# Three moved steps in a gated mix of linear attention and single-expert retrieval: the last transposed coefficients, wo's last low part, and tile 1's sums of w

## The chip, the core and the metric

One NeuronCore of a Trainium2 chip runs the whole kernel. Its engines work side by side, each through its own instructions in order: TensorE (PE: matmuls out of SBUF into PSUM; PEld is its weight load), VectorE (DVE), ScalarE (ACT), GpSimd (POOL), and SyncE (SP), which here only issues DMAs. They wait for one another through semaphores. The metric is the device time of one execution in microseconds (us); less is better.

## The reference

For 2048 rows `x` of 512 numbers, two branches are mixed by a gate. `A_w_phi` is drawn 200 times larger than its plain scale.

```python
# A: linear attention, 32 heads of 16
q, k, v = split(x @ wqkv)
phi = lambda p: concat([softmax(p), softmax(-p)])     # 32 features
phi_q, phi_k = phi(q @ w_phi), phi(k @ w_phi)
kv = einsum("bhsf,bhsd->bhfd", phi_k, v);  z = sum_s(phi_k)
a = (phi_q @ kv / (phi_q . z + 1e-6)) @ wo
# B: 256 experts = 16 x 16, the best one per head
s1, s2 = q1 @ k1.T, q2 @ k2.T                         # per row and head
e = argmax(s1) * 16 + argmax(s2)
b = sum_over_heads( gelu(x . u[e]) * v[e] )           # softmax over one candidate is 1
g = sigmoid((x * gate_w).sum())
out = g * a + (1 - g) * b
```

As all heads share the experts' tables, `b` is, for each row, a count C of how often each of the 256 experts is chosen, times G = (1 - g) gelu(x . u), times the table `v`.

## The kernel before

**Tiles.** Rows are worked on in 16 tiles of 128 (a = 0 to 15). Numbers that go through a matmul are split into a high and a low part (`xh`/`xl`, `woh`/`wol`, `eh`/`el`, `ch`/`cl`), and three matmuls (high-high, high-low, low-high) make one product.

**Stages.** A first stage, up to about a third of the time, makes keys, values and the sums over all rows. The second is a software pipeline, written out by hand (`manual_schedule`: each engine takes its work in the order of the text). Pass a of the loop at L972 does the query softmax of tile a, the counting of tile b = a - 1 and the output of tile z = a - 2, and starts the scores of tile n = a + 1. The last tiles are written out behind the loop (L1080 to L1137).

**The steps by name.**

- `soft_in(a)` (L115 to L121, VectorE): the differences to maximum and minimum of the query projection; `soft_exp(a)` (L685, ScalarE): two exponentials; `soft_w(a)` (L691, POOL): w = phi times `zb`, two halves; `soft_sum(a, i)` (L695, VectorE): sums of phi; `soft_y(a, i)` (L705, VectorE): sums of w; `soft_p(a)` (L700, VectorE); `soft_b(a)` (L713 to L726): the factors on VectorE, with one step of a's own counting between each two of them, and the final products on POOL (L726). `planes` (L758), a DMA transpose and `join` (L768) turn phi; `mid_num` (L777, L781) makes the numerator and copies its high part to `xh`; `num_lo` (L788) makes the low part.
- `best(n, half)` (L734, L735, VectorE): row maximum of the scores and the places that equal it; `turn_eq`: their DMA transpose; `mid_mask` (L796, TensorE): bit masks of them.
- `count(t)` (L800): a generator of VectorE operations that turns the masks into C. `step(t, n)` runs the next n of its yields, `drain(t)` all that are left. L804 to L808 are the first five, L812 and L814 the sixth, L822 the seventh, L825 the eighth, and L826 to L836 follow.
- `gelu_in` (L653, POOL), `gelu_act` (L657 to L659, ScalarE), `gelu_out` (L663, POOL) make G. `coef` (L840) multiplies C by G, on POOL for all but the last two tiles. `c_planes` (L845, ScalarE, then a DMA transpose from SP) and `c_join` (L852, L856, ScalarE) turn the product and leave `ch`; `back_cl` (L877) makes `cl`. For the last two tiles `back_c` (L866, L868, L872) turns it on TensorE.
- `back(z)` runs `back_mm` (L882): 12 matmuls of the numerator with `woh`/`wol` (L889) and then 6 of the coefficients with `eh`/`el` (L896), into one bank `po`; `store` copies it out (L913) and writes it by DMA.

**`wo`.** `woh` and `wol` hold four parts each, in memory that earlier tables used (L879). Part 3 goes where `wbh` and `wbl`, the weights of `vproj`, lie, so it can be written only after `vproj(15)` in pass a = 1: its high part on ScalarE (L984), its low part on VectorE (L1005). Part 2's low part is on POOL (L1043).

**Order around the change, pass a = 1.** VectorE: `soft_in(1)`, L1005, three steps of tile 0's counting (L812 to L825), `best(2, 0)`, the two `soft_sum(1)`, the rest of tile 0's counting (L826 to L836), the two `soft_y(1)`, `soft_p(1)`, `soft_b(1)`. POOL: `soft_b(0)`'s products (L726), `gelu_in(1)`, `soft_w(1)`, `gelu_out(0)`, `coef(0)`. ScalarE: the planes of tile 0, `soft_exp(1)`, the copies of `kvb` (L919), `join(0)`, `c_planes(0)`, `gelu_act(1)`, and then in pass a = 2 the `xh` copies of tile 0, `gelu_pre(2)` and `c_join(0)` among tile 1's planes.

**Order at the end.** Tile 15's output is made in two halves of 256 columns, `end0` and `end1`, each with 12 matmuls L889 and 6 matmuls L896. All 24 L889 come first, then `back_c(15)`'s two transposes, ScalarE's `ch`, VectorE's `cl`, then the L896 of either half, with a copy and a DMA behind each.

Of the kernel before, what the change touches and what calls it, by code (L numbers as in the profile page):

```python
# [16 lines left out]
ALU = mybir.AluOpType  # L17
# [18 lines left out]
def mix_kernel(ctx, tc, xT, wqT, wkT, wv, wphi, wo, wq, kk, ug, ev, cst, out):  # L36
    nc = tc.nc
    pe, dve, act, pool, sp = nc.tensor, nc.vector, nc.scalar, nc.gpsimd, nc.sync
# [4 lines left out]
    def mm_bank(name):  # L43
        return psum.tile([P, 512], F32, tag="mm", bufs=4, name=name)
# [206 lines left out]
    def vproj(t, ks=range(NK)):  # L251
        pv = mm_bank(f"pv{t}")
        proj(pv, t, wbh, wbl, 0, D, ks)
        v = v_tile(t)
        return lambda: act.copy(v, by16(pv))
# [134 lines left out]
    def spare(src, name, shape):  # L390
        t_ = wa_.tile(shape, F32, tag="xr", bufs=4, name=name)
        sp.dma_start(t_, src)
        return t_
# [75 lines left out]
    for t in range(5, NT - 1, 2):  # L469
        n = t + 1  # L470
# [13 lines left out]
        a = pks[t] = mm_bank(f"pk{t}")  # L484
        prod(a, tile_of(t, 0), b11, True)
        b = mm_bank(f"pu{t}")
# [97 lines left out]
    rawo = {k: spare(wo[:, k], f"rawo{k}", [P, D]) for k in range(2)}  # L584
# [28 lines left out]
    def step(t, n=1):  # L613
        for _ in range(n):
            if t in chains and next(chains[t], None) is None:
                del chains[t]

    def drain(t):
        while t in chains:
            step(t)  # L620
# [22 lines left out]
    def gelu_pre(t):  # L643
        gelu_gate(t)
        gelu_rest(t)

    def gate(t):
        gs = st8[t]["g"]
        yield dve.reciprocal(gs[:, 2:3], gs[:, 1:2])

    def gelu_in(t):
        px, x2 = st8[t]["G"], st8[t]["x2"]
        pool.tensor_tensor(x2, x2, px, op=ALU.mult)  # L653
# [11 lines left out]
    def front_q(t):  # L665
        pq = mm_bank(f"pq{t}")
        proj(pq, t, wah, wal, 0, D)
        st8[t]["pq"] = pq
# [13 lines left out]
    def soft_exp(t):  # L682
        d = st8[t]["ph"]
        for i in range(2):
            act.activation(hs(d, i), hs(d, i), AF.Exp)  # L685
# [11 lines left out]
    def soft_p(t):  # L697
        st = st8[t]["st"]
        sm = pair(st[:, 64:128])
        dve.scalar_tensor_tensor(st[:, 128:224].rearrange("p (h c) -> p h c", c=3)[:, :, 2], sm[:, :, 0], 1e-6,  # L700
                                 sm[:, :, 1], op0=ALU.mult, op1=ALU.mult)
# [52 lines left out]
    def planes(t, i):  # L754
        e = st8[t]
        e.setdefault("tp", [])
        pl = w3.tile([P, 2, 512], U16, tag="pl", name=f"pl{i}_{t}")
        act.copy(pl, e["ph"][:, halves[i]].bitcast(U16).rearrange("p (c j) -> p j c", j=2))  # L758
        tp = w3.tile([P, 8, P], U16, tag="tp", name=f"tp{i}_{t}")
        sp.dma_start_transpose(tp, pl.rearrange("p j c -> p (j c)"))  # L760
        e["tp"].append(tp)
# [9 lines left out]
    def mid_num(t):  # L771
        e = st8[t]
        o = [tr_bank(f"oT{q}_{t}") for q in range(2)]
        for g in range(8):
            for q in range(2):
                r0, c0 = 64 * q, 32 * (g % 4)
                pe.matmul(o[q][c0:c0 + 32, (g // 4) * P:(g // 4 + 1) * P], kvb[r0:r0 + 64, g, :],  # L777
                          e["pt"][r0:r0 + 64, g, :], start=(g < 4), stop=True, skip_group_check=True)
        oh, ol = x_of(t)
        for q in range(2):  # L780
            act.copy(oh[:, 2 * q:2 * q + 2].rearrange("p k n -> p (k n)"), o[q][:, :2 * P])  # L781
        e["o"] = (oh, ol, o)

    def num_lo(t):
        oh, ol, o = st8[t]["o"]
        for q in range(2):
            k2 = lambda a: a[:, 2 * q:2 * q + 2].rearrange("p k n -> p (k n)")
            dve.tensor_tensor(k2(ol), o[q][:, :2 * P], k2(oh), op=ALU.subtract)  # L788
# [60 lines left out]
    def c_join(t):  # L849
        e = st8[t]  # L850
        tj = w4.tile([P, 2 * P], F32, tag="ctj", bufs=1, name=f"ctj{t}")
        act.copy(tj.bitcast(U16).rearrange("p (k n j) -> p j k n", j=2, n=P),  # L852
                 e["tc"].rearrange("p (j k) n -> p j k n", j=2))
        ch = w4.tile([P, 2 * P], F32R, tag="ch", name=f"ch{t}")
        cl = w4.tile([P, 2 * P], F32R, tag="cl", name=f"cl{t}")
        act.copy(ch, tj)  # L856
        if t == 0:
            w4.tile([P, 120], F32, name="rest4", bufs=1)
        e["c"] = (ch, cl, tj)
# [15 lines left out]
    def back_cl(t, eng=dve):  # L875
        ch, cl, o = st8[t]["c"]
        eng.tensor_tensor(cl, o[:, :2 * P], ch, op=ALU.subtract)  # L877

    woh, wol = ([a[:, 0], a[:, 1], b.rearrange("p k n -> p (k n)"), c[:, 0]]  # L879
                for a, b, c in ((t1h, gh, wbh), (t1l, gl, wbl)))  # L880
# [20 lines left out]
    def back(t, n=18):  # L901
        if t not in backs:
            split_ = DEFER - 2 <= t < NT - 3
            e = st8[t]
            e["po"] = psum.tile([P, 512], F32, tag="acc", name=f"po{t}") if split_ else mm_bank(f"po{t}")
            backs[t] = back_mm(t, bank=e["po"])
        for _ in range(n):
            next(backs[t])

    def store(t):  # L910
        po = st8.pop(t)["po"]
        ot = w3.tile([P, D], F32, tag="ot", name=f"ot{t}")
        act.copy(ot, po)  # L913
        sp.dma_start(out[t * P:(t + 1) * P, :], ot)
# [57 lines left out]
    for a in range(NT - 1):  # L972
        n, b, z = a + 1, a - 1, a - 2
        owed = min(18, 3 * max(0, a - DEFER))
        left = min(18, 3 * max(0, a - DEFER + 1))
        B, Z = b >= 0, z >= 0
        if Z:
            mid_num(z)
        if a == 2:
            gelu_pre(a)  # L980
        if a == 1:
            front_q(a)
            v15 = vproj(NT - 1)
            act.copy(woh[3], rawo[3])  # L984
        if B:
            planes(b, 0)
            if Z:
                c_join(z)
            if a == 1:
                v15()  # L990
            planes(b, 1)
        if a > 1:
            front_q(a)
        if owed:
            back(z - 1, owed)
            store(z - 1)
        gelu_in(a)
        if Z:
            num_lo(z)
        if B:  # L1000
            if a == 1:
                for _ in gate(a):
                    pass
                soft_in(a)
                dve.tensor_tensor(wol[3], rawo[3], woh[3], op=ALU.subtract)  # L1005
                step(b, 3)
            else:
                soft_in(a, dealt(a, b, z))
                drain(b)
        else:  # L1010
            for _ in gate(a):
                pass
        if a != 1:
            gelu_act(a)
        if a > 0:
            soft_exp(a)
        if Z and not left:
            back(z)
            store(z)
        if not left and a > 1:  # L1020
            mid_mask(a)
        if a:
            front_s(n, 0)
        if left or a == 1:
            mid_mask(a)
            if 0 < left < 18:
                back(z, 18 - left)
        if a == 1:
            kvacc(NT - 1)
            kv_final()  # L1030
            cl_.close()
            w4 = ctx.enter_context(tc_pool("w4", "right"))
        front_s(n, 1)
        front_p(n, False)
        soft_w(a)
        if a == 1:
            best(n, 0)
        soft_sum(a, 0)
        soft_sum(a, 1)
        if a == 1:  # L1040
            drain(b)
        if a == 0:
            pool.tensor_tensor(wol[2], rawo[2], woh[2], op=ALU.subtract)  # L1043
            step(a, 5)
        if a != 1:
            best(n, 0)
        if a == 0:
            best(n, 1)
            turn_eq(n)
        soft_y(a, 0)  # L1050
        soft_y(a, 1)
        soft_p(a)
        if B:
            join(b)
            gelu_out(b)
            coef(b)
            c_planes(b)
            if a == 1:
                gelu_act(a)
        if a == 0:  # L1060
            soft_b(a, lambda t: None)
        else:
            soft_b(a)
            best(n, 1)
            turn_eq(n)
        if a != 1:
            gelu_pre(n)
    a, b, z = NT - 1, NT - 2, NT - 3
# [19 lines left out]
    for _ in gate(a):  # L1088
# [34 lines left out]
    coef(a)  # L1123
    ends = [(back_mm(a, slice(256 * i, 256 * i + 256), o[:, :256]), o) for i, o in
            enumerate((mm_bank("end0"), mm_bank("end1")))]
    for g, _ in ends:
        for _ in range(12):
            next(g)
    back_c(a)
    back_cl(a)  # L1130
    ot = w3.tile([P, D], F32, tag="ot", name="ot_end")
    for i, (g, o) in enumerate(ends):
        for _ in range(6):
# [57 lines left out]
```

## Time and profile before

| | |
|---|---|
| time, median of 3 executions | 373.98 us (373.77 to 374.05) |
| the profiled execution | 373.71 us |
| its span in the profile | 371.9 us, 8839 instructions |
| TensorE busy | 365.0 us (98%) |
| VectorE busy | 332.6 us (89%) |
| ScalarE busy | 256.3 us (69%) |
| POOL busy | 203.1 us (55%) |
| chain that ended last | PE 83%, DVE 5%, POOL 3%, ACT 3%, issue 3%, DMA 2% |

The profile comes from one execution. A row of the timeline gives the start in us from the start of the span, the duration in us, the engine, the line, the operation, what it writes and reads, how many instructions are merged in it, and in brackets how long the engine was idle before and what ended that. A row's duration counts any time in which the operation had begun and was held up, so a row longer than others of its kind is a sign of a hold-up. Neighbouring rows of one engine may overlap by some hundredths of a microsecond, as instructions are pipelined; ends of matmuls are modelled. The span ends when the last output transfer has landed, some 2 us behind the last instruction; the execution's time is 1.8 us longer than the span.

### The profile page before, as it was taken

Reading aid. Unit: us, or ns where it says so; the run is one execution under the profiler, and the core shown is the slowest. Engines: PE = TensorE matmul, PEld = TensorE weight load, DVE = VectorE, ACT = ScalarE, POOL = GpSimd, SP = SyncE. Lnnn points to the kernel's source line nnn. Section 1 sums busy time; section 2 is a strip of 40 time slices with the busy share of each in tenths; the row PEclk is TensorE's granted clock in tenths of the full one; section 3 lists DMA queues with packets and bytes.
Section 4 is the critical chain, followed back from the end, with each engine's and each line's share of the span. In section 5 each row is a group of like instructions: output and inputs, shape, how many; then the busy total and the mean of one; then the engine's idle time right before and its main releaser. Section 6 shows DMA issues by size and latency. Waiting matters only on the chain.

```text
span 371.9 us, 8839 instructions
## 1 busy us (share of the span) xinstructions
PE 365.0 (98%) x3443; PEld 286.2 (77%) x3443; DVE 332.6 (89%) x786; ACT 256.3 (69%) x459; POOL 203.1 (55%) x205
## 2 busy tenths in 40 slices
PE   8999999999999999999999999999999999999995
PEld 4766767777878878777888888878878888888875
DVE  3679999999787979999989999999999999999993
ACT  4585577876666676677868659667786786777641
POOL 1079989988848846443634436426435445454700
PEclk9999999999999999999999999999999999999999
DMA  7868987557882304145264242351452532532201
GB/s 259 321 241 277 252 278 237 173 179 277 279 179 85 89 6 82 24 105 82 61 86 104 57 95 75 85 100 16 114 76 67 115 77 66 115 69 62 70 31 56
DMA packets 72074, 46.67 MB, mean 125 GB/s; under 512 B 63584, under 2 KB 64480, under 8 KB 69728
## 3 DMA queue, kind: packets, MB, share of 16 engines
q1 hardware_dynamic: 71168, 45.24, 45.5%
q10 hardware_dynamic: 864, 0.87, 0.9%
q8 instruction: 27, 0.44, 0.5%
q14 instruction: 15, 0.12, 0.1%
HBM read 26.43 MB, written 4.19 MB: 82 GB/s over the span
## 4 chain that ended last, share of the span: by engine, by line
PE 83%; DVE 5%; POOL 3%; ACT 3%; issue 3%; DMA 2%; SPq 0%; POOLq 0%; ACTq 0%; DVEq 0%
PE po L889 10%; PE s L56 7%; PE s L57 6%; PE s L58 6%; PE po L896 6%; PE pk L459 5%; PE pu L459 4%; PE ws L292 4%; PE pq L56 4%; PE pq L58 3%; PE pq L57 3%; PE oT L777 2%; PE pe L459 2%; PE kvacc L283 2%; PE pv L459 2%
## 5 line engine op out<-in xcount | busy, mean ns | idle before, releaser
L691 POOL TENSOR_TENSOR w<-d,zb 128x512 f32<-128x512 f32 x32 | 40.9, 1297 | 76.8 <-ACT d L685 76.8
L56 PE MATMUL s<-sh,xh 128*128 128x512 f32 x128 | 50.9, 397 | 0.0
L57 PE MATMUL s<-sl,xh 128*128 128x512 f32 x128 | 49.9, 390 | 0.0
L58 PE MATMUL s<-sh,xl 128*128 128x512 f32 x128 | 49.8, 389 | 0.0
L726 POOL TENSOR_TENSOR d<-d,st 128x512 f32<-128x512 f32 x30 | 31.2, 1062 | 28.1 <-DVE st L720 26.5
L685 ACT ACTIVATE d<-d 128x512 f32<-128x512 f32 x32 | 20.0, 632 | 34.2 <-DVE d L119 26.1
L276 POOL TENSOR_TENSOR d<-d,st 128x1024 f32<-128x1024 f32 x16 | 32.5, 2032 | 8.5 <-ACT d L267 6.6
L768 ACT COPY pt<-tp 128x1024 uint16<-128x1024 uint16 x28 | 36.3, 1369 | 0.0
L758 ACT COPY pl<-d 128x1024 uint16<-128x1024 uint16 x28 | 29.2, 1044 | 5.5 <-POOL d L726 5.4
L58 PEld LDWEIGHTS s<-sh,xl 128*128 128x128 f32 x128 | 24.0, 188 | 5.0
L56 PEld LDWEIGHTS s<-sh,xh 128*128 128x128 f32 x128 | 24.0, 188 | 4.7
L57 PEld LDWEIGHTS s<-sl,xh 128*128 128x128 f32 x128 | 24.1, 188 | 4.6
L56 PE MATMUL pq<-wah,xh 128*128 128x512 f32 x64 | 26.8, 418 | 0.0
L58 PE MATMUL pq<-wah,xl 128*128 128x512 f32 x64 | 25.1, 392 | 0.0
L57 PE MATMUL pq<-wal,xh 128*128 128x512 f32 x64 | 25.0, 390 | 0.0
L156 DVE TENSOR_TENSOR xl<-xr,xh 128x512 fp32r<-128x512 f32 (+2 forms) x17 | 21.7, 1288 | 1.7 <-ACT xh L152 1.6
L735 DVE TENSOR_TENSOR eq<-s,mx 128x512 bf16<-128x512 f32 x32 | 22.1, 691 | 1.1
L695 DVE TENSOR_REDUCE st<-d 128x32 f32<-128x512 f32 x32 | 21.5, 680 | 1.4
L734 DVE TENSOR_REDUCE mx<-s 128x32 f32<-128x512 f32 x32 | 21.8, 680 | 0.0
L705 DVE TENSOR_REDUCE st<-w 128x32 f32<-128x512 f32 x32 | 20.5, 677 | 0.6 <-POOL w L691 0.6
L271 DVE TENSOR_REDUCE st<-d 128x64 f32<-128x1024 f32 x16 | 19.4, 1209 | 1.8 <-ACT d L267 1.6
L267 ACT ACTIVATE d<-d 128x1024 f32<-128x1024 f32 x16 | 17.1, 1066 | 4.1 <-DVE d L121 4.1
(272 smaller groups left out, 1119.3 us busy)
## 6 DMA issues: line engine op xcount, KB each, us to landing
wq<-wq SPq DMA_DIRECT2D x16, 1024.0 KB, 5.8
xr<-xT SPq DMA_DIRECT2D x15, 256.0 KB, 5.1
y<-ot SPq DMA_DIRECT2D x15, 256.0 KB, 2.3
rawk<-wkT SPq DMA_DIRECT2D x1, 1024.0 KB, 6.5
rawq<-wqT SPq DMA_DIRECT2D x1, 1024.0 KB, 6.8
rawu<-ug SPq DMA_DIRECT2D x2, 258.0 KB, 5.2
rawv<-wv ACTq DMA_DIRECT2D x2, 256.0 KB, 4.7
rawv<-wv SPq DMA_DIRECT2D x2, 256.0 KB, 5.9
```

What stands on the lines that cost most here:

```text
L56: pe.matmul(o, ah, bh, start=(first and i == 0), stop=False)
L57: pe.matmul(o, ah, bl, start=False, stop=False)
L58: pe.matmul(o, al, bh, start=False, stop=(last and i == n - 1))
L276: pool.tensor_tensor(g64(d), g64(d), b64(st[:, 128:192]), op=ALU.mult)
L459: pe.matmul(o, x_, w_, start=(first and i + j == 0), stop=(i == 1 and j == 2), skip_group_check=True)
L691: pool.tensor_tensor(hs(e["w"], i), hs(e["ph"], i), hs(zb, i), op=ALU.mult)
L726: eng.tensor_tensor(g64(d)[:, gs_], g64(d)[:, gs_], r[:, gs_].unsqueeze(2).to_broadcast([P, 32, F]), op=ALU.mult)
L735: dve.tensor_tensor(e["eq"][:, 512 * half:512 * half + 512].rearrange("p (h f) -> p h f", f=F), p3, mx.unsqueeze(2).to_broadcast([P, H, F] ...
L758: act.copy(pl, e["ph"][:, halves[i]].bitcast(U16).rearrange("p (c j) -> p j c", j=2))
L768: act.copy(p16[:, :, 4 * i:4 * i + 4, :], e["tp"][i].rearrange("p (j g) n -> p j g n", j=2))
L889: pe.matmul(po, a, b, start=(i == 0), stop=False)
L896: pe.matmul(po, a, b, start=False, stop=(i == 5))
```

## The change

Three places, all of them moves of work that stays the same:

1. In pass a = 1, the low part of `wo`'s part 3 is made by POOL instead of VectorE, at the same place in the text: on POOL that is behind `gelu_in(1)` and ahead of `soft_w(1)`.
2. In pass a = 1, the rest of tile 0's counting (`drain(b)`) is moved from behind `soft_sum(1)` to behind `soft_y(1)` and `soft_p(1)`. It stays ahead of `join(0)`, `gelu_out(0)` and `coef(0)` in the text; these are on other engines.
3. At the end, the transposes of tile 15's coefficients, and ScalarE's and VectorE's work on them, come behind 18 of the 24 matmuls L889 instead of behind all 24; the remaining six, which belong to `end1`, follow the transposes on TensorE.

```diff
@@ -1002,7 +1002,7 @@
                 for _ in gate(a):
                     pass
                 soft_in(a)
-                dve.tensor_tensor(wol[3], rawo[3], woh[3], op=ALU.subtract)
+                pool.tensor_tensor(wol[3], rawo[3], woh[3], op=ALU.subtract)
                 step(b, 3)
             else:
                 soft_in(a, dealt(a, b, z))
@@ -1037,8 +1037,6 @@
             best(n, 0)
         soft_sum(a, 0)
         soft_sum(a, 1)
-        if a == 1:
-            drain(b)
         if a == 0:
             pool.tensor_tensor(wol[2], rawo[2], woh[2], op=ALU.subtract)
             step(a, 5)
@@ -1050,6 +1048,8 @@
         soft_y(a, 0)
         soft_y(a, 1)
         soft_p(a)
+        if a == 1:
+            drain(b)
         if B:
             join(b)
             gelu_out(b)
@@ -1123,11 +1123,13 @@
     coef(a)
     ends = [(back_mm(a, slice(256 * i, 256 * i + 256), o[:, :256]), o) for i, o in
             enumerate((mm_bank("end0"), mm_bank("end1")))]
-    for g, _ in ends:
-        for _ in range(12):
+    for (g, _), n in zip(ends, (12, 6)):
+        for _ in range(n):
             next(g)
     back_c(a)
     back_cl(a)
+    for _ in range(6):
+        next(ends[1][0])
     ot = w3.tile([P, D], F32, tag="ot", name="ot_end")
     for i, (g, o) in enumerate(ends):
         for _ in range(6):
```

## The prediction

> **What bounds the kernel now.** I first read which waits TensorE has at all, since its instructions run in the order written and it is busy for nearly the whole span. The view of waits, for TensorE alone, has five rows; three lie where the change touches the program (columns: who waits for whom, us in total, times, longest).
>
> ```profile
> PE po L889 <- ACT xh L781: 0.6, 1, 0.6
> PE po L896 <- ACT ch L856: 0.6, 1, 0.6
> PE end L896 <- ACT ch L872: 0.5, 1, 0.5
> ```
>
> The first two are in pass a = 2 (tile 0's output matmuls), the third at the very end. Everywhere between them TensorE waits for nobody, so a microsecond won or lost at one of these places should reach the end whole. What sets the first is in the chain of work that ended last, cut to that window (start, us, what):
>
> ```profile
> 152.01 0.44 DVE cf L836
> ...
> 152.61 0.75 POOL cf L840
> 153.38 0.62 ACT plc L845
> ...
> 155.07 0.65 ACT xh L781 x2
> ```
>
> ```profile
> 155.50 0.50 PE L889 MATMUL po<-t1h,xh 128*128 128x512 f32 x1 [0.61 <-ACT xh L781]
> ```
>
> The chain reads backwards: TensorE's `po` matmul needs ScalarE's copies `xh`. ScalarE takes its work in order too, so these copies stand behind `plc`, tile 0's `c_planes`; that waits for POOL's product L840, and this for L836, the last step of tile 0's counting on VectorE. So the end of the counting, at 152.45, sets TensorE's restart at 155.50. The wait for `ch` stands behind the same ScalarE work and moves with it.
>
> VectorE and POOL before that, from the timeline (start, us, engine, line):
>
> ```profile
> 143.50 0.67 DVE L121 TENSOR_TENSOR d<-st,pq 128x512 f32<-128x512 f32 x1
> 144.09 1.19 DVE L1005 TENSOR_TENSOR wbl<-rawo,wbh 128x512 fp32r<-128x512 f32 x1
> 145.21 0.21 DVE L812 TENSOR_TENSOR m<-sa 128x64 uint16<-128x64 uint16 x1
> 145.34 0.17 DVE L814 TENSOR_TENSOR m<-sa 128x32 uint16<-128x32 uint16 x1
> 145.54 0.43 DVE L822 TENSOR_TENSOR X<-m,m 128x256 uint32<-128x256 uint32 x1
> 146.00 0.29 DVE L825 TENSOR_SCALAR T<-X 128x256 uint32<-128x256 uint32 x1
> 146.21 0.68 DVE L734 TENSOR_REDUCE mx<-s 128x32 f32<-128x512 f32 x1
> ...
> 147.54 1.27 DVE L695 TENSOR_REDUCE st<-d 128x32 f32<-128x512 f32 x2
> 148.72 0.96 DVE L826 TENSOR_TENSOR X<-X,T 128x512 uint16<-128x512 uint16 x1
> ...
> 152.35 1.27 DVE L705 TENSOR_REDUCE st<-w 128x32 f32<-128x512 f32 x2
> ...
> 153.64 0.22 DVE L804 CAST sa<-mk 128x64 uint16<-128x64 f32 x1
> ```
>
> ```profile
> 139.13 1.28 POOL L1043 TENSOR_TENSOR gl<-rawo,gh 128x512 fp32r<-128x512 f32 x1
> ...
> 144.00 0.74 POOL L653 TENSOR_TENSOR x<-x,px 128x256 f32<-128x256 f32 x1
> 146.13 2.56 POOL L691 TENSOR_TENSOR w<-d,zb 128x512 f32<-128x512 f32 x2 [1.40 <-ACT d L685]
> 148.66 0.74 POOL L663 TENSOR_TENSOR px<-x,px 128x256 f32<-128x256 f32 x1
> ```
>
> VectorE has no idle time here, and two of its rows are too long: L1005 and L826. Each began while a POOL product was running (L653, L663) and ended shortly after it.
>
> **How the two engines block each other.** L1005 ends at 145.28, 0.54 after L653's end (144.74). L826 ends at 149.68, 0.28 after L663's end (149.40); its usual duration is the first number here:
>
> ```profile
> L826 DVE TENSOR_TENSOR X<-X,T x16: 424/426/960, 148.7 to 361.3; 128x512 uint16<-128x512 uint16 x16
> ```
>
> So a VectorE operation with two SBUF inputs waits for the POOL operation under way, and then needs its own duration less about 0.15 (0.43 - 0.28). Who comes next when both queue is shown early in the kernel; the last two rows give the lines' usual durations (ns: least, median, most):
>
> ```profile
> 37.75 3.03 DVE L156 TENSOR_TENSOR xl<-xr,xh 128x512 fp32r<-128x512 f32 x2
> 37.79 2.44 POOL L276 TENSOR_TENSOR d<-d,st 128x1024 f32<-128x1024 f32 x1
> 40.19 1.74 POOL L316 TENSOR_TENSOR sl<-wtj,sh 128x512 fp32r<-128x512 f32 x1
> ```
>
> ```profile
> L276 POOL TENSOR_TENSOR d<-d,st x16: 1932/1942/2470, 30.7 to 126.1; 128x1024 f32<-128x1024 f32 x16
> ```
>
> ```profile
> L316 POOL TENSOR_TENSOR sl<-wtj,sh x8: 1270/1295/1736, 40.2 to 119.0; 128x512 fp32r<-128x512 f32 x8
> ```
>
> The first L156 runs and L276 is 0.50 longer than its median; the second L156 waits for L276 and ends 0.55 after it (40.78 against 40.23); L316 is again 0.44 too long. They take turns, one instruction each, and whoever is waiting goes next.
>
> **Part 1: wol[3] on POOL.** VectorE loses L1005, 1.19. POOL gains one operation of L1043's shape and kinds, 1.28, between L653 and L691, where POOL is idle for 1.40 (144.74 to 146.13): alone, it would hide there. But three steps of tile 0's counting now follow `soft_in` directly, from 144.10, and L812, L814 and L822 each have two SBUF inputs. Step by step:
>
> - L812 waits for L653 and goes in at 144.74; 0.21 - 0.15 = 0.06, so it is done at 144.80. Then wol[3] has its turn, 1.28, to 146.05 or so (POOL rows overlap by some 0.03).
> - L814, next on VectorE, waits for that and is done at 146.07 (0.17 - 0.15). L822 begins 0.03 behind it, at 146.10, by a hair ahead of L691's 146.13. It takes its 0.43, to 146.53, and holds L691 up by some 0.20: the first L691 (1.28) ends at 147.61.
> - L825 comes at 146.55 and meets that L691. It has one input. No row shows such an operation beside POOL. Reductions with one input (L695 inside L691's 2.56) aren't lengthened: wait 0 is the lower end. The upper end is the two-input rule: to 147.61, then 0.29 - 0.15, done at 147.75. I take the upper end: L825 writes as many 32-bit elements as L822 in 0.29 instead of 0.43, on the same tile in SBUF, so it moves more than one per cycle, unlike the reductions (0.68 for 512), and needs more than one way to memory.
> - L734, best(2,0), begins 0.08 before L825's end, at 147.67 (146.21 now). Had nothing blocked, it couldn't begin before the scores, 145.66 + 0.39 = 146.05 below, so the removed 1.19 is worth 0.1 at most:
>
> ```profile
> 145.66 0.39 PE L58 MATMUL s<-sh,xl 128*128 128x512 f32 x1
> ```
>
> For L825 the Trainium skill, SBUF — State Buffer, section Who interferes with whom, says that tensor_scalar can enter a mode that uses both of VectorE's SBUF ports and then blocks with GpSimd for a whole instruction. By that rule the upper end is right and the sum is as below; by the reductions' rows it would be 0.95 less. The same section says that what issues first wins, which fits L653 and L812; the turns after it are from the rows above.
>
> **Part 2: the sums of w ahead of the rest of the counting.** From L734 to the end of the second L695 is 2.51 (146.21 to 148.72) and stays. Now come the two sums of w and `soft_p`: from L705's start to that of L804 behind them, 1.29. They don't wait: w's halves are written by about 147.6 and 148.9, and the sums start at 147.67 + 2.51 = 150.18. So L826 starts at 151.47. POOL's L663 is then over, and L826 takes 0.43 instead of 0.96: it ends at 151.90, against 149.68. From there the counting is as before: L836 ends, and L840, `plc`, `xh` and TensorE's L889 start, 2.22 later. The pieces: 1.46 (L734 late) + 1.29 (sums first) - 0.53 (L826 unblocked).
>
> Queued behind the late L840 on POOL are only tile 1's products L726, which wait for VectorE's steps behind the counting; these are late by less than 2.2, as VectorE's work between has become shorter. Behind `plc` on ScalarE stand `gelu_act(1)`, the `xh` copies, `gelu_pre(2)`, tile 1's planes with their transposes, and `c_join`, all late by 2.22, as TensorE is. No DMA is added or removed; the transpose of `plc` starts later by the same. **+2.22**.
>
> **Part 3: the last coefficients.** The end, from the timeline:
>
> ```profile
> 364.53 0.43 DVE L840 TENSOR_TENSOR cf<-cf,px 128x256 f32<-128x256 f32 x1
> 365.17 0.28 PE L889 MATMUL end<-gl,xh 128*128 128x256 f32 x1
> 365.89 0.28 PE L889 MATMUL end<-wbh,xl 128*128 128x256 f32 x1
> 366.01 0.38 PE L866 MATMUL CT<-cs,cf 128*128 128x128 f32 x2
> 366.49 0.37 ACT L872 CAST ch<-CT 128x256 fp32r<-128x256 f32 x1 [2.52 <-PE CT L866]
> 366.89 0.42 DVE L877 TENSOR_TENSOR cl<-CT,ch 128x256 fp32r<-128x256 f32 x1 [1.93 <-ACT ch L872]
> 366.91 0.39 PE L896 MATMUL end<-eh,ch 128*128 128x256 f32 x1 [0.52 <-ACT ch L872]
> 367.13 0.28 PE L896 MATMUL end<-el,ch 128*128 128x256 f32 x1
> ...
> 368.69 0.37 ACT L1136 COPY ot_end<-end 128x256 f32<-128x256 f32 x1 [1.83 <-PE end L896]
> ```
>
> The row at 365.17 is the 18th of the 24 matmuls, that at 365.89 the last: (365.89 - 365.17) / 6 = 0.12 each. The transposes go from 366.01 to 365.29; their input, L840, is done at 364.96, 0.33 earlier. Then `ch` goes to 365.77-366.14 and `cl` to 366.17-366.59. Six matmuls, 0.72, now fill what was the wait. Eight transposes elsewhere took 1.04:
>
> ```profile
> 357.87 1.04 PE L749 MATMUL pt<-cs,d 128*128 128x128 f32 x8
> ```
>
> So two take 0.26 of TensorE (their own row has 0.38, the upper end). L896 can begin at 365.29 + 0.26 + 0.72 = 366.27, behind `ch` (366.19 with its 0.05 of signal), and its second matmul at 366.39 instead of 367.13: 0.74 (0.62 by the upper end, never above 0.72 and the 0.10 that the restart costs, 367.13 - 366.91 against 0.12). The matmuls with `cl` come fifth, at 366.75, after 366.59. Copies and output DMAs behind move along. **-0.74**.
>
> **Sum.** +2.22 - 0.74 = +1.48. The profiled execution took 373.71 (span 371.9): 375.19. The median shown, 373.98, is 0.27 above it, so **375.5** on that scale.
>
> **Rivals.**
>
> *Worse turns.* L822 beats L691 by 0.03 of estimate. If L691 wins, L822 waits to 147.41 and is done at 147.69; the second L691 is held up and ends at 148.85, L825 at 148.99, L734 begins at 148.91: 1.24 more, +2.7, 376.7. For it: the hair's breadth; against it: if L814 slips in with L812, L822 waits for wol[3] alone and goes at its end, 146.05, clear of L691.
>
> *L825 doesn't wait.* L734 begins at 146.55 + 0.21 = 146.76, 0.91 earlier: +0.5 to +0.6, 374.5. For it: the one-input reductions; against it: the pace.
>
> *Blocking doesn't bite on such short steps* (the side that isn't slower). L812, L814 and L822 slip between L653 and wol[3], and wol[3] hides in POOL's 1.40. L734 begins at 146.10, L826 at 149.90, ending at 150.33: +0.65, and with the end -0.09: 373.9. It decides from the point where L734 begins before 146.2. Against it: the turns at 37.75 and L812's own 0.06, too short to keep POOL's next operation out for three instructions.
>
> *The end doesn't move.* If the last transposes wait for L840 past 366.0, part 3 gives nothing: +2.2, 376.2. Against it: 0.33 of margin.
>
> *Faster* would need the front to lose nothing, TensorE's restart at 155.50 not hanging on L836: -0.74, 373.2. Against it: ScalarE's `plc` starts 0.02 after L840's end.
>
> **How the numbers follow.** The forecast has 0.50 (with it the case that L814 slips in with L812: 0.1 less), worse turns 0.15, L825 not waiting 0.14, no blocking 0.10, the end not moving 0.05, faster 0.06. Differences within 0.2% (0.75 us) can't be told from none here. Faster: 0.06. Same: no blocking and most of L825 not waiting, 0.22. Slower: the rest, 0.72. The range, 374.2 to 376.9, takes in L825's two ends, the worse turns without a slower clock, and the end's 0.62 to 0.82; left out are no blocking and faster, 0.16.
>
> **What would show it.** In the new trace: L812 ending with L653, L814 some 1.2 later with wol[3], L825 stretched to about 1.2 beside L691; L826 at 0.43 and starting near 151.5; ScalarE idle before `plc` 2.2 longer; TensorE's wait for `xh` at 2.8 instead of 0.61. At the end, no wait before L896 and the last copy 0.7 earlier relative to the 18th matmul. I'm wrong if L734 begins before 147, or if TensorE's wait for `xh` stays under 1.5.

## The result, and the profile after

| | before | after |
|---|---|---|
| time, median of 7 executions each | 373.93 us (373.57 to 374.16) | 375.45 us (374.86 to 377.33) |
| ratio, with its 95% interval | | 1.0048 (1.0029 to 1.0067) |
| the profiled execution | 373.71 us | 374.91 us |
| its span | 371.9 us | 373.1 us |

The kernel became slower by about half a per cent, 1.5 us by the medians. The two profiled executions differ by 1.2. The changed kernel's seven executions also lie farther apart, and three of them (375.78, 376.08, 377.33) show a mean granted TensorE clock of 0.994 instead of 1.000; this turned out to belong to the change.

The waits of TensorE in the changed kernel (who waits for whom, us, times, longest):

```profile
PE po L889 <- ACT xh L781: 2.8, 1, 2.8
...
PE po L896 <- ACT ch L856: 0.6, 1, 0.6
```

The wait at the end has gone from the list; the one in pass a = 2 has grown from 0.6 to 2.8. VectorE in pass a = 1 (start, us, engine, line), where the reader is to compare the durations of L812, L814 and L825 with the 0.21, 0.17 and 0.29 of before:

```profile
143.37 0.68 DVE L121 TENSOR_TENSOR d<-st,pq 128x512 f32<-128x512 f32 x1
143.96 0.71 DVE L812 TENSOR_TENSOR m<-sa 128x64 uint16<-128x64 uint16 x1
144.60 1.29 DVE L814 TENSOR_TENSOR m<-sa 128x32 uint16<-128x32 uint16 x1
145.92 0.43 DVE L822 TENSOR_TENSOR X<-m,m 128x256 uint32<-128x256 uint32 x1
146.38 1.26 DVE L825 TENSOR_SCALAR T<-X 128x256 uint32<-128x256 uint32 x1
147.56 0.68 DVE L734 TENSOR_REDUCE mx<-s 128x32 f32<-128x512 f32 x1
...
150.07 1.27 DVE L705 TENSOR_REDUCE st<-w 128x32 f32<-128x512 f32 x2
...
151.35 0.42 DVE L826 TENSOR_TENSOR X<-X,T 128x512 uint16<-128x512 uint16 x1
...
154.10 0.42 DVE L836 TENSOR_TENSOR cf<-X 128x256 f32<-128x256 uint8 x1
```

and POOL beside it, where each long row of VectorE finds its partner:

```profile
143.86 0.73 POOL L653 TENSOR_TENSOR x<-x,px 128x256 f32<-128x256 f32 x1
144.55 1.30 POOL L1005 TENSOR_TENSOR wbl<-rawo,wbh 128x512 fp32r<-128x512 f32 x1
146.00 2.80 POOL L691 TENSOR_TENSOR w<-d,zb 128x512 f32<-128x512 f32 x2 [0.15 <-ACT d L685]
148.75 0.75 POOL L663 TENSOR_TENSOR px<-x,px 128x256 f32<-128x256 f32 x1
154.67 0.72 POOL L840 TENSOR_TENSOR cf<-cf,px 128x256 f32<-128x256 f32 x1 [5.17 <-DVE sa L804]
```

L812 ends at 144.67, with L653 (144.59). L814 ends at 145.89, with L1005, which is wol[3] (145.85). L822 slips in ahead of L691 and makes that pair 2.80 long instead of 2.56. L825 waits for the first product of that pair and ends at 147.64. All later steps of the counting keep their old durations, L826 now has its normal one, and the counting ends at 154.52 instead of 152.44. (The bracket of the L840 row names L804, which began while L836 was ending; the product's input is written by L836.)

The end (TensorE, ScalarE), where 367.08 is the 18th of the 24 matmuls and nothing waits any more:

```profile
367.08 0.28 PE L889 MATMUL end<-gl,xh 128*128 128x256 f32 x1
367.20 0.38 PE L866 MATMUL CT<-cs,cf 128*128 128x128 f32 x2
367.34 0.36 PE L889 MATMUL end<-wbh,xh 128*128 128x256 f32 x1
...
368.13 0.35 PE L896 MATMUL end<-eh,ch 128*128 128x256 f32 x1
368.32 0.28 PE L896 MATMUL end<-el,ch 128*128 128x256 f32 x1
...
369.87 0.37 ACT L1138 COPY ot_end<-end 128x256 f32<-128x256 f32 x1 [1.83 <-PE end L896]
```

From the 18th matmul to the second L896 it is 1.24 us, against 1.96 before (367.13 - 365.17): 0.72 won.

### The profile page after: what moved, and what is told of

Read it like the earlier page. It is cut to its first block, busy times and chain, and to the rows that moved or that the text cites. A ratio compares the mean times of both kernels' runs of the same rounds, so it can differ in the third digit from the quotient of the medians.

```text
span 373.1 us, 8838 instructions
## 1 busy us (share of the span) xinstructions
PE 364.9 (98%) x3443; PEld 286.1 (77%) x3443; DVE 334.9 (90%) x785; ACT 256.6 (69%) x459; POOL 205.7 (55%) x206
## 4 chain that ended last, share of the span: by engine, by line
PE 83%; DVE 5%; POOL 3%; ACT 3%; issue 3%; DMA 1%; ACTq 0%; POOLq 0%
PE po L889 10%; PE s L56 7%; PE s L57 6%; PE s L58 6%; PE po L896 6%; PE pk L459 5%; PE pu L459 4%; PE ws L292 4%; PE pq L56 4%; PE pq L58 3%; PE pq L57 3%; PE oT L777 2%; PE pe L459 2%; PE kvacc L283 2%; PE pv L459 2%
## 5 line engine op out<-in xcount | busy, mean ns | idle before, releaser
L691 POOL TENSOR_TENSOR w<-d,zb 128x512 f32<-128x512 f32 x32 | 41.1, 1304 | 75.4 <-ACT d L685 75.4
L58 PE MATMUL s<-sh,xl 128*128 128x512 f32 x128 | 49.9, 390 | 0.0
L58 PEld LDWEIGHTS s<-sh,xl 128*128 128x128 f32 x128 | 24.0, 188 | 5.1
L58 PE MATMUL pq<-wah,xl 128*128 128x512 f32 x64 | 25.1, 392 | 0.0
L156 DVE TENSOR_TENSOR xl<-xr,xh 128x512 fp32r<-128x512 f32 (+2 forms) x17 | 21.7, 1288 | 1.7 <-ACT xh L152 1.6
L734 DVE TENSOR_REDUCE mx<-s 128x32 f32<-128x512 f32 x32 | 21.8, 681 | 0.0
```

The source lines that it names most:

```text
L58: pe.matmul(o, al, bh, start=False, stop=(last and i == n - 1))
L691: pool.tensor_tensor(hs(e["w"], i), hs(e["ph"], i), hs(zb, i), op=ALU.mult)
```

## The experiments

Executions of one kernel differ by up to 3 us on the chips of the experiments (the kernel before: 373.16 to 375.97), partly from a wait ahead of the loop: TensorE's for x15's low part (`pk L58 <- DVE xl L156`), 1.2 us in the profiled executions of some kernels (part 1 alone, the longer wait, the changed kernel again, and two of the last versions) and none in others. So beside the time I read two distances in each trace that this wait doesn't enter: from the start of L121 (the last difference of `soft_in(1)`) to the start of L836 (the counting's last step), and from L121 to TensorE's L889. The column of waits gives TensorE's for `xh`, the last column the executions with a mean clock below 0.997.

| kernel | L121 to L836 | L121 to L889 | wait for xh | median, its ratio (interval) | low clock |
|---|---|---|---|---|---|
| before | 8.51 | 12.00 | 0.6 | 373.9 to 374.0 | 0 of 68 |
| changed | 10.73 | 14.16 | 2.8 | 375.45, 1.0048 (1.0029 to 1.0067) | 3 of 7 |
| part 3 alone | 8.51 | 11.98 | 0.6 | 373.30, 0.9990 (0.9974 to 1.0006) | 0 of 12 |
| part 1 alone | 9.44 | 12.89 | 1.5 | 375.61, 1.0047 (1.0032 to 1.0063) | 0 of 6 |
| part 2 alone | 9.25 | 12.80 | 1.4 | 374.73, 1.0019 (1.0005 to 1.0033) | 0 of 12 |
| parts 1 and 2 | 10.73 | 14.17 | 2.8 | 376.96, 1.0098 (1.0076 to 1.0119) | 5 of 6 |
| changed, L825 later | 9.77 | 13.22 | 1.8 | 374.78, 1.0017 (0.9999 to 1.0035) | 8 of 12 |
| changed, longer wait | 11.92 | 15.35 | 4.0 | 378.63, 1.0110 (1.0076 to 1.0143) | 4 of 4 |
| changed, again | 10.74 | 14.17 | 2.8 | 376.25, 1.0048 (1.0027 to 1.0069) | 8 of 12 |

**Each part alone, and the first two together.** The edits are hunks of the change, put into the kernel before.

> Part 3 alone. Theory (the loss is all in pass a = 1 and the end gains): 0.7 less than the kernel before, ratio 0.998; TensorE's wait for xh at L889 stays at 0.6, the last ch no longer makes L896 wait. Rival (the end's gain is given back in the tail, or the change's loss comes from the end): ratio 1.000 or above. If the executions with a granted clock of 0.994 belong to the long wait in pass a = 2, none is seen here.

> Part 1 alone: wol[3] on POOL, the counting where it was. Theory (the engines take turns): L814 and L825 take about 1.2 each, L734 begins 1.46 later than in the kernel before, L826 then meets no POOL product and takes 0.43 instead of 0.96; its end and TensorE's restart at L889 are 0.9 later (wait for xh 1.5), time +0.9. Rival (no blocking of such short steps, POOL hides wol[3] for nothing): L734 0.1 earlier, L826 still 0.96, time -0.1 to 0.

> Part 2 alone: the sums of w ahead of the rest of tile 0's counting, wol[3] on VectorE. Theory: L826 begins 1.29 later but takes 0.43 instead of 0.96, so the counting ends 0.76 later; wait for xh 1.4, time +0.75. Rival (the order of the sums carries the whole loss of the change, wol[3] on POOL none): time +2, wait for xh 2.8.

> Parts 1 and 2 without the end. Theory: both share the one gain of 0.53 at L826, so together they cost 0.53 more than the sum of the parts alone: 0.93 + 0.76 + 0.53 = 2.2; wait for xh 2.8, time +2.0 in executions with a granted clock of 1.00. Rival (the parts simply add): +1.7. If the wait of 2.8 is what brings the clock below 1.00, some executions show 0.99 and are 1 to 2 us longer still, as in the changed kernel, and the parts alone (waits of 1.4 to 1.5) show none.

Part 3 alone leaves pass a = 1 as it was (8.51) and takes 0.57 off the median; its interval there reaches just over 1, and with the repetition below (0.9973, 0.9956 to 0.9990) the gain is clear. Part 1 alone makes the counting end 0.93 later (9.44 - 8.51), as expected to the hundredth: L814 takes 1.28 and L825 1.25 in that trace, L734 begins 1.49 later counted from L121, and L826 takes 0.41. Its median is higher than that by 0.8 (375.61 - 373.87 = 1.74 against 0.93). In the profiled execution the excess lies ahead of pass a = 1: it reached L121 1.49 later than the kernel before (144.99 against 143.50), 1.2 of it the early wait, and 373.71 + 1.49 + 0.89 (the restart, 12.89 - 12.00) is 376.09 where it took 376.06. Whether the same holds for the other five (374.88 to 376.37) isn't known, as only one execution has a trace. Part 2 alone costs 0.74 in the trace and 0.7 to 0.9 in the time (1.0019 of 374, and 374.73 - 373.87). Together the parts cost 2.22 at L836, 0.55 more than 0.93 + 0.74: each of them alone moves L826 out from under L663 and gains that 0.53, but it can be gained only once. The rivals, that POOL hides wol[3] for nothing, that the order of the sums carries the whole loss or that the parts simply add, fall by the traces.

The last of the four also showed what the prediction hasn't: with the wait at 2.8, five of six executions had a clock of 0.990 to 0.995, and none of the thirty with waits up to 1.5. (The sixth, at a full clock, took 376.19, 2.3 more than the kernel before, where 2.0 was expected.)

**L825, the step with one input.**

```diff
-                step(b, 3)
+                step(b, 2)
```

> The changed kernel, but only two steps of tile 0's counting (to L822) ahead of best(2, 0); L825, the step with one input, goes behind the sums with the rest. Theory (L825 lost about 1 us beside the first product L691, not by itself): L734 begins 1.1 earlier than in the changed kernel, L825 takes 0.29 in its new place, so L836 ends 0.8 earlier; wait for xh 2.0; time 0.8 less than the changed kernel's 374.9 in executions at a clock of 1.00. Rival (L825 cost only its place in the order): L734 0.2 to 0.3 earlier and the counting's end where it was, wait 2.8, time as the changed kernel. With a wait of 2.0 no execution shows a clock below 0.998.

```profile
144.15 1.28 DVE L814 TENSOR_TENSOR m<-sa 128x32 uint16<-128x32 uint16 x1
145.47 0.43 DVE L822 TENSOR_TENSOR X<-m,m 128x256 uint32<-128x256 uint32 x1
145.81 0.69 DVE L734 TENSOR_REDUCE mx<-s 128x32 f32<-128x512 f32 x1
...
149.60 0.29 DVE L825 TENSOR_SCALAR T<-X 128x256 uint32<-128x256 uint32 x1
```

Out from beside L691, L825 takes 0.29 instead of 1.26, and the counting ends 0.96 earlier (9.77 against 10.73; 0.8 was expected). So the step with one input did wait for POOL's product, and its place in the order is not what it cost. The same expectation had two misses. The four executions at a full clock took 374.6 in the median, some 0.5 less than those of the changed kernel (375.15 in the first comparison, 375.1 below), where 0.8 was expected. And with a wait of 1.8, eight of the twelve executions show a low clock. TensorE in this kernel's profiled execution, one of these eight:

```profile
153.91 0.39 PE L58 MATMUL pq<-wah,xl 128*128 128x512 f32 x1
156.13 0.65 PE L889 MATMUL po<-t1h,xh 128*128 128x512 f32 x1 [1.83 <-ACT xh L781]
156.57 0.63 PE L889 MATMUL po<-t1l,xh 128*128 128x512 f32 x1
157.00 0.63 PE L889 MATMUL po<-t1h,xh 128*128 128x512 f32 x1
...
160.11 0.40 PE L889 MATMUL po<-gh,xl 128*128 128x512 f32 x1
160.34 0.39 PE L889 MATMUL po<-wbh,xl 128*128 128x512 f32 x1
...
161.96 0.36 PE L796 MATMUL mk<-wm,et 128*128 128x16 bf16 x8
```

and the same stretches with their granted clock (the column behind the x counts of POOL):

```profile
154.00:156.00 2.00, 0.30 (x2) 0.00 (x0) 1.97 (x10) 1.92 (x6) 0.88 (x1) 1.00 0.06 14
156.00:158.00 2.00, 1.87 (x5) 1.49 (x6) 2.00 (x7) 1.94 (x8) 1.46 (x3) 0.58 0.40 90
158.00:160.00 2.00, 2.00 (x7) 1.57 (x6) 1.86 (x5) 1.97 (x4) 0.51 (x1) 0.57 0.50 110
160.00:162.00 2.00, 2.00 (x12) 1.43 (x11) 1.93 (x6) 1.65 (x4) 0.00 (x0) 1.00 0.65 126
```

Behind the pause the matmuls start 0.43 apart instead of 0.23, for some 3.5 us; then the clock is back. The next group of matmuls, L796 (the bit masks), shows the price. In the changed kernel's profiled execution, at a full clock, it has this row:

```profile
162.66 0.36 PE L796 MATMUL mk<-wm,et 128*128 128x16 bf16 x8
```

From the restart to L796 that is 5.13 at a full clock (162.66 - 157.53) and 5.83 here (161.96 - 156.13): 0.70 more. The first ten matmuls alone lose 1.56 (160.11 - 156.13 = 3.98, against 159.95 - 157.53 = 2.42); the rest is regained because TensorE, slower, no longer waits for `ch` behind them.

**A longer wait, and the changed kernel again.**

```diff
         if a == 1:
+            for i in (0, 1):
+                soft_y(a, i)
             drain(b)
```

> The changed kernel with both sums of w of tile 1 made twice, which puts 1.2 more of VectorE's time in front of the rest of tile 0's counting: TensorE's wait for xh 4.0 instead of 2.8. Theory (the lower clock follows the length of this wait): every execution, or nearly so, shows a granted clock below 0.998, and the time is 1.2 above the changed kernel's for the wait and 1 to 2 more for the clock, 377 to 378.5; the profile shows the matmuls behind the wait at twice their spacing of 0.23. Rival (the clocks of 0.994 belong to the chip or the moment, not to the wait): clock 1.00 in most executions and 1.2 more, 376.1.

> The changed kernel once more beside the others, on their chip. Theory: executions at a clock of 1.00 take about 1.2 more than the kernel before, some show 0.994 and take 1 to 2 more; ratio 1.003 to 1.007. Rival (the first comparison's spread was chance): all at 1.00, ratio 1.003 with little spread.

The wait of 4.0 has a low clock in all four executions (0.990 to 0.995). Their median, 378.63, lies just above the expected 377 to 378.5. The clock falls behind the wait:

```profile
156.00:160.00 4.00, 0.10 (x1) 0.00 (x0) 3.86 (x16) 1.98 (x6) 1.66 (x2) 1.00 0.05 11
160.00:162.00 2.00, 1.93 (x6) 1.54 (x7) 2.00 (x7) 1.94 (x8) 1.46 (x3) 0.68 0.40 90
162.00:164.00 2.00, 2.00 (x7) 1.52 (x6) 1.86 (x6) 1.97 (x4) 0.46 (x1) 0.50 0.49 107
```

Of the changed kernel's twelve, eight had it (median 376.5) and four not (median 375.1). So the low clock belongs to the pause and not to a chip or a moment: none in 68 executions of the kernel before, in three series, none at 1.5 and less, most from 1.8 on (34 of 47). Its price is 0.7 in the two traces that can be compared (5.83 above, and 5.84 behind the wait of 4.0, against 5.13). The medians of executions with and without it differ by 0.5 (L825 later), 0.9 (376.1 - 375.2, the first comparison) and 1.4 (376.5 - 375.1, here), in small groups that can differ in the early wait as well.

**A version meant to beat both.** From the kernel with part 3 alone, against which the code below is shown, and from the reading above: keep POOL's products away from the counting's steps, and do more of the counting where VectorE waits for the scores.

```diff
     act.copy(woh[2], rawo[2])
+    pool.tensor_tensor(wol[2], rawo[2], woh[2], op=ALU.subtract)
...
-        gelu_in(a)
+        if a != 1:
+            gelu_in(a)
...
-                dve.tensor_tensor(wol[3], rawo[3], woh[3], op=ALU.subtract)
-                step(b, 3)
+                step(b, 6)
...
         if a == 0:
-            pool.tensor_tensor(wol[2], rawo[2], woh[2], op=ALU.subtract)
+            gelu_pre(n)
+            gelu_out(a)
+            gelu_in(n)
             step(a, 5)
...
         soft_y(a, 1)
+        if a == 1:
+            dve.tensor_tensor(wol[3], rawo[3], woh[3], op=ALU.subtract)
         soft_p(a)
...
-            gelu_out(b)
+            if b:
+                gelu_out(b)
...
-        if a != 1:
+        if a > 1:
             gelu_pre(n)
```

and `back_cl(0)` one step earlier in `dealt`.

> A version meant to beat both: the end as changed; in pass a = 1 no POOL product beside the counting's steps. wol[2] on POOL right behind its high part; gelu_out(0) and gelu_in(1) on POOL in its old place, ahead of soft_b(0); wol[3] on VectorE between soft_y(1) and soft_p(1); six steps of tile 0's counting (to L828) ahead of best(2, 0), where VectorE waits for the scores anyway; the rest of the counting ahead of the sums of w as before; back_cl(0) one place earlier. Theory (the front is bound by the end of the counting): L836 ends 1.8 earlier than in the kernel before, TensorE's waits for xh (0.6) and ch (0.6) go to 0 to 0.2, with the end 0.7: 1.7 to 1.9 less than before, ratio 0.995. Rival (the wait moves: the products L726 or cl come late in turn): only the end's 0.7, ratio 0.998.

It failed: 378.02, 1.0093 (1.0063 to 1.0123), though the counting ended nearly as early as expected (6.86 from L121, 1.65 less). ScalarE shows why:

```profile
148.20 1.06 ACT L919 COPY kvb<-kvacc 32x128 f32<-32x128 f32 x4 [0.31 <-PE kvacc L283]
153.96 2.53 ACT L768 COPY pt<-tp 128x1024 uint16<-128x1024 uint16 x2 [4.70 <-issue]
```

```profile
153.20 0.68 DVE L1058 TENSOR_TENSOR wbl<-rawo,wbh 128x512 fp32r<-128x512 f32 x1
```

`join(0)` stands still for 4.70 and starts at 153.96, 0.08 after wol[3] ends on VectorE. (`issue` in the bracket means that the profile shows no releaser; that it is wol[3] rests on these times, on the memory, and on the mended version below.) In the kernel's text the memory of `rawo`'s parts 2 and 3 (the pool `late`, on the right side) is given back right before the pool `w4`, from which `pt` comes, is opened on the same side, so that `pt` can lie over it: wol[3] must be done before `join(0)` may write. It has a deadline that none of its own readers sets. TensorE paused 2.8 for it at L777, and all six executions had a low clock. The mended version puts wol[3] back behind `soft_in(1)` on VectorE and takes `step(b, 4)`:

> The version before, with wol[3] back in its old place on VectorE (behind soft_in(1), so that its source is free before join(0) writes over it) and four steps of tile 0's counting (to L826) ahead of best(2, 0). Theory (join(0) waited for wol[3], because pt lies over rawo's memory; the front is otherwise bound by the counting's end): ScalarE doesn't wait before L768; L1005 takes 0.69 instead of 1.19; L836 ends 1.0 earlier than in the kernel before; TensorE's wait for xh is 0, that for ch 0.6 at an earlier time: 1.0 less there and 0.7 at the end, ratio 0.9955, no clock below 0.998. Rival (join(0) waited for the transposes of tile 0's planes): its wait stays above 2, time as the version before or near it.

```profile
143.97 0.68 DVE L1009 TENSOR_TENSOR wbl<-rawo,wbh 128x512 fp32r<-128x512 f32 x1
...
145.70 0.43 DVE L826 TENSOR_TENSOR X<-X,T 128x512 uint16<-128x512 uint16 x1
146.04 0.68 DVE L734 TENSOR_REDUCE mx<-s 128x32 f32<-128x512 f32 x1
148.55 0.28 DVE L827 TENSOR_SCALAR T<-X 128x256 uint32<-128x256 uint32 x1
...
150.84 0.42 DVE L836 TENSOR_TENSOR cf<-X 128x256 f32<-128x256 uint8 x1
```

wol[3] takes 0.68 where it took 1.19, as L653 no longer runs beside it (it is over at 140.39); the counting ends 1.05 earlier (7.46 from L121), ScalarE doesn't wait before `join(0)`, and TensorE's wait for `xh` is gone. 372.53, 0.9958 (0.9937 to 0.9979). With `c_join(0)` also ahead of tile 1's planes:

```diff
         if B:
+            if z == 0:
+                c_join(z)
             planes(b, 0)
-            if Z:
+            if z > 0:
                 c_join(z)
```

> The same, with c_join(0) ahead of tile 1's first planes on ScalarE. Theory (what is left is ScalarE's chain to ch): the wait for ch goes to 0.1 or none, 0.5 less than the version without it, ratio 0.994. Rival (the transpose of the coefficients lands too late, or tile 1's planes then come late for join(1)): no gain, and a wait at L777 in its place.

> Part 3 alone once more, beside the two versions above. Theory: 0.7 less than the kernel before, ratio 0.998, and 1.0 and 1.5 more than the two. Rival (the versions' gain is only the end's): the three equal.

372.03, 0.9934 (0.9907 to 0.9960): the wait for `ch` is gone too, and TensorE runs through there.

```profile
158.73 0.39 PE L889 MATMUL po<-wbh,xl 128*128 128x512 f32 x1
158.96 0.39 PE L896 MATMUL po<-eh,ch 128*128 128x512 f32 x1
```

Part 3 alone, beside them, had 373.31, 0.9973 (0.9956 to 0.9990). The steps of the medians, 0.8 and 0.5, are near the expected 1.0 and 0.5; the two versions' own intervals overlap, so that the last step is shown by its trace more than by its time.

## Why the prediction was right

The median, 375.45, is within 0.1 of the predicted 375.5, with the sign at the likeliest chance. Point by point:

- **The place.** TensorE restarts when ScalarE's copies come, and these when the counting ends. Confirmed in every kernel with `join(0)` in time and the counting as late as before or later: L121 to L889 moves with L121 to L836 (8.51/12.00, 9.25/12.80, 9.44/12.89, 10.73/14.16, 11.92/15.35).
- **Part 1, L734 1.46 late.** Measured 1.48 counted from L121 (147.56 - 143.37 against 146.21 - 143.50). The turns came as worked out, L822's narrow win over L691 included.
- **L825's two ends.** The upper one held: L825 took 1.26 in the trace and 0.29 when it was moved, and the counting then ended 0.96 earlier. The Trainium skill's rule (SBUF — State Buffer, Who interferes with whom), that tensor_scalar can take both ports and then blocks with GpSimd, agrees with that 1.26. The reductions' rows, the ground for the lower end, didn't carry over to it. (What the lower end would have taken off is 0.91 by the prediction's own steps, 147.67 - 146.76, and not the 0.95 that stands beside the rule.)
- **Part 2, and the sum in front, +2.22.** The counting ended 2.22 later counted from L121 (10.73 - 8.51). TensorE's restart came 2.16 later on the same count, 2.03 on the span's clock, as this execution reached pass a = 1 0.13 sooner.
- **Part 3, -0.74.** Measured -0.72.
- **The total, +1.48.** Between the profiled executions it is +1.20, 0.28 less. 0.13 of that is the earlier arrival at pass a = 1, and 0.06 the restart (2.16 for 2.22). Another 0.12 is won back between the restart (2.03 late) and the 18th of the last matmuls (1.91 late): 0.06 where TensorE had paused for `cl` in pass a = 2, the rest a pass later. Then the end takes off its 0.72, which leaves 1.19.

What the prediction lacked is the clock: it has no term for it. At a full clock the change costs about 1.2 by the first comparison (374.91 against 373.71 in the profiled executions; 375.15 against 373.93 by the medians, with the three executions at a low clock left out) and 1.0 by the repetition (375.1 against 374.0). The three executions at a low clock lift the first median by 0.3, to 375.45. So the mechanism was right step by step, but that the figure came within 0.1 is luck: by its own working it would have been some 0.3 too high. The rivals with their own mechanisms (worse turns, L825 not waiting, no blocking, the end not moving, nothing lost in front) are all contradicted by the trace.

## What to carry to other kernels

Before work is moved to an idle engine, list what else runs beside it that reads the same way: here 1.28 us on an idle POOL set three short steps of VectorE against POOL's products, one each, and made them 2.59 us longer in all (0.50 + 1.12 + 0.97), where VectorE was relieved of 1.19. Cost two edits together, since both can claim the same stall only once. And a step's deadline may be set by whoever takes over the memory of its source, which is seen in the pools, not in its readers.

## What the runs showed of the hardware beyond that

A TensorE wait of 1.8 us was followed by a lower clock in eight of twelve executions; with waits up to 1.5 it never was (0 of 30, and 0 of 68 before the change). The Trainium skill, TensorE: Matmul & The Clock Gate, Part 1, gives about 3.4 us of idle time for that; the rows here show it after less.

How long the clock stays down can be read from the windows' clock column, as it went to half (0.50 in windows that it fills): behind the wait of 1.8, (0.42 + 0.43) x 2 us x 2 = 3.4 us, from about the restart; behind the wait of 4.0 the same 3.4 (0.68, 0.50 and 0.97), from some 0.7 after the restart. The failed version's profiled execution, whose TensorE stopped at 152.57 and restarted at 155.35, had twice that:

```profile
154.00:156.00 2.00, 0.65 (x16) 0.23 (x16) 2.00 (x11) 2.00 (x2) 0.47 (x1) 0.72 0.00 0
156.00:158.00 2.00, 1.48 (x23) 0.97 (x19) 0.78 (x2) 1.97 (x5) 1.60 (x2) 0.50 0.04 8
158.00:160.00 2.00, 2.00 (x6) 1.52 (x6) 0.76 (x2) 1.91 (x9) 0.00 (x0) 0.50 0.52 119
160.00:162.00 2.00, 2.00 (x7) 1.57 (x6) 0.00 (x0) 1.97 (x4) 0.73 (x1) 0.57 0.35 78
```

(0.28 + 0.50 + 0.50 + 0.43) x 2 us x 2 = 6.8 us, and counted back from 156.00 it began at about 154.9, with TensorE still waiting, 2.3 after it had stopped (an estimate from these rows). Its mean clock is 0.991, where the two others have 0.995 and 0.994. At one and the same wait of 2.8 some executions had a low clock and some not, so the length isn't all that decides; what else does was not tried.

The blocking reached one more place than was worked out. In the changed kernel's timeline VectorE has

```profile
154.71 0.73 DVE L805 TENSOR_TENSOR sb<-sa 128x64 uint16<-128x64 uint16 x1
```

beside POOL's L840 (154.67 to 155.39), which now follows the counting while VectorE is at tile 1's steps; in the kernel before L805 took 0.19 there. Nothing in the waits of TensorE hangs on it, as TensorE was later still.
